# Hash attention and a gated feed-forward block on one core: the first pair of heads is begun in one sweep, and the up products take both halves of the columns under one block of weights

## The chip, the cores and the metric

The kernel runs on one core of one Trainium2 chip. The metric is the device time of one launch in microseconds (us). A core has engines that run their own instruction streams side by side: TensorE (PE in the profile, with the loads of its weights shown apart as PEld), VectorE (DVE), ScalarE (ACT), GpSimd (POOL) and SyncE (SP). Transfers run on 16 DMA engines. SP, ACT and POOL issue them, each into a queue of its own.

## The reference

```python
# attention: batch 4, heads 8, sequence 768, head size 64, 6 hash bits
q_bucket = sum_i ((q @ proj)[..., i] > 0) * 2**i        # k_bucket likewise
scores = where(q_bucket == k_bucket, q @ k.T / 8, -1e9)
attn = exp(scores - max(scores)); attn = attn / (sum(attn) + 1e-9)
x = (attn @ v), heads side by side                      # 3072 x 512
# gated block: d_ff 1536
out = (silu(x @ w_gate) * (x @ w_val)) @ w_out          # 3072 x 512
```

A query attends only to keys that have the same six sign bits.

## The kernel before, in words

**Attention.** Two heads form a pair, and there are 16 pairs, worked one after the other. A pair holds q and k transposed in tiles `qT` and `kT` (128 x 768: two heads of 64 rows each) and their sign bits in `qb` and `kb` (bf16). The 768 queries are two halves of 384 columns, the 768 keys six chunks of 128. A *unit* is one half of the queries against one chunk of keys, for both heads; a pair has 12. `score(u)` takes two PSUM banks, one for each head, and puts two kinds of products in them: `kT` by `qT` (fp32, each product two passes of the array) and on top of these `kb` by `qb` (bf16). The bit product is the mask: the scale is chosen so that only keys with equal bits survive the exponential. Two ACT instructions (L506) then write exp of the unit into `A`. After all 12 units `attend` multiplies `A` with v (L517), and DVE adds the units up for the row sums (L538, L542, L545, called by `add`). `total` sums these over the keys a pair later; the sums go through memory (`few`, `sums`, `r`; SP issues them at L561, L567, L574) and come back as factors.

**Bits.** `hash_blocks` multiplies `hash_w` with `qT` or `kT` (L435) into a bank `hps`, each block of 384 columns in its own 32 rows, and ACT takes the sign (L440). `spread_k` writes the k bits for both heads (L449, two DVE instructions); the q bits are copied to the second head's rows by DVE (L462, first pair) or by a DMA of POOL (L452, later pairs).

**How a pair is prepared.** For the pairs after the first, DVE transposes both operands in 32 x 32 blocks (L473), one pair ahead; for the first, TensorE transposes in 128 x 128 blocks (L422) and ACT copies them out of PSUM (L425). The first pair's preparation is eight steps in a list: transpose k half 0, transpose q half 0, hash k half 0, hash q half 0, and the same for the halves 1. The first four run before any unit. Between the two kinds of products of unit 0 one step runs, between those of unit 1 two more, and after unit 2 the last one. `raw` tiles that q and k are loaded into have one buffer each: the next pair's load waits for this pair's transposes.

**Queues at the start.** SP issues q half 0, k half 1, v, q half 1; ACT issues k half 0; POOL issues `proj`. POOL also clears three bit tiles (L407), and nine idle products (L367) run on TensorE meanwhile. `TURN` (8) is the unit of the first pair after which the second pair's transposes go into DVE's stream and the third pair's loads into SP's.

**PSUM.** Attention has eight banks handed out in turn: a new tile takes the bank of the eighth tile before it and waits for that one's readers.

**Weights.** Between attention's own work the feed-forward weights are split in three parts of few bits each (`begin_pieces`, `advance_pieces`: ACT L135 to L142, DVE L149 to L164). They go to memory and come back in `ring` tiles.

**Gated block.** Three blocks of 1024 tokens, and for each 12 *up* steps and 4 *down* steps. An up step does gate and value: `first` makes 16 products of 128 x 512 into the two banks of `a`, `second` eight into the two banks of `n` (all by `mm`, L669). Each product is a weight load and a matmul. The two banks are the two halves of the tokens (`half`, 512 columns each); ACT or DVE reads both in one instruction of 1024 columns (L708, L714). The order of everything is the order in which the program is written; no planner moves it.

Of the kernel before, what the change touches and what calls it, by code (L numbers as in the profile page):

```python
# [19 lines left out]
def kernel(  # L20
# [20 lines left out]
    nc = tc.nc  # L41
# [256 lines left out]
    def attention(scope):  # L298
# [13 lines left out]
        def fetch(n, name, queue, half=None):  # L312
            b, pr = pairs[n]
            if name == "v":
                t = raws["v", n] = raw.tile([P, 2, NCH, D], FP32, tag="vraw", name="vraw")
                queue.dma_start(
                    t.rearrange("p h c d -> p h (c d)"),
                    v[b, 2 * pr : 2 * pr + 2].rearrange("h (p c) d -> p h (c d)", c=NCH),
                )
                return  # L320
            src = q if name == "q" else k
            if not half:
                raws[name, n] = raw.tile([P, NCH, 2, D], FP32, tag=name + "raw", name=name + "raw",
                                         bufs=1)
            t = raws[name, n]
            if n == 0:
                cs = slice(None) if half is None else slice(half * CH, (half + 1) * CH)
                for h in range(2):
                    queue.dma_start(t[:, cs, h, :],
                                    src[b, 2 * pr + h].rearrange("(p c) d -> p c d", c=NCH)[:, cs, :])  # L330
                return
            blocks = t.rearrange("p c a b -> p (c a b)").rearrange(
                "p (c a d) -> p c a d", a=P // BLOCK, d=BLOCK)
            for h in range(2):
                for x in range(D // BLOCK):
                    at = h * D + x * BLOCK
                    queue.dma_start(
                        blocks[at : at + BLOCK],
                        src[b, 2 * pr + h][:, x * BLOCK : (x + 1) * BLOCK].rearrange(
                            "(a p c) d -> p c a d", c=NCH, p=BLOCK))  # L340
# [6 lines left out]
        two_proj = fixed.tile([P, NBITS], FP32, tag="proj", name="proj")  # L347
        for o in (0, D):
            nc.gpsimd.dma_start(two_proj[o : o + D, :], proj[:, :])
        fetch(0, "q", nc.sync, 0)  # L350
        fetch(0, "k", nc.scalar, 0)
        fetch(0, "k", nc.sync, 1)
        fetch(0, "v", nc.sync)
        fetch(0, "q", nc.sync, 1)

        ident = fixed.tile([P, P], FP32, tag="ident", name="ident")
        make_identity(nc, ident)
# [4 lines left out]
                sides[name, i] = fixed.tile([P, S], BF16, tag=name + f"b{i}", name=name + "b")  # L362
        zeros = sides["k", 1]
        nc.vector.memset(zeros, 0.0)
        for _ in range(9):
            ps = bank("idle")
            nc.tensor.matmul(ps, zeros[:, 0:P], zeros[:, 0:512], start=True, stop=True)  # L367
# [35 lines left out]
            nc.gpsimd.memset(t.rearrange("p u h q -> p (u h) q")[:, :, HQ:AW], 1.0)  # L403
            twos.append(t)
        ring = [t[:, i] for t in twos for i in range(2)]
        for t in (sides["k", 0], sides["q", 0], sides["q", 1]):
            nc.gpsimd.memset(t, 0.0)  # L407

        for name in "kqv":
            fetch(1, name, nc.sync)  # L410
# [3 lines left out]
        bits = {}  # L414

        def front(n):
            def transpose(name, half):
                if (name, n) not in T:
                    T[name, n] = opnd.tile([P, S], FP32, tag=name + "T", name=name + "T")
                ps = bank("tps")  # L420
                for i in range(CH):
                    nc.tensor.transpose(ps[:, i * P : (i + 1) * P],  # L422
                                        raws[name, n][:, half * CH + i, :, :].rearrange("p h d -> p (h d)"),
                                        ident)
                nc.scalar.activation(T[name, n][:, half * HQ : (half + 1) * HQ], ps[:, 0:HQ], AF.Copy,  # L425
                                     scale=2 / OFF if name == "k" else 1.0)

            bits["q", n] = sides["q", n % 2]
            bits["k", n] = sides["k", n % 2]
            low, high = slice(0, BLOCK), slice(D, D + BLOCK)  # L430

            def hash_blocks(todo):
                tile_ = bank("hps")
                for i, (name, half) in enumerate(todo):
                    nc.tensor.matmul(tile_[i * BLOCK : (i + 1) * BLOCK, 0:HQ], hash_w,  # L435
                                     T[name, n][:, half * HQ : (half + 1) * HQ],
                                     start=True, stop=True)

                def sign(i, name, half, to=low, **how):
                    nc.scalar.activation(bits[name, n][to, half * HQ : (half + 1) * HQ],  # L440
                                         tile_[i * BLOCK : (i + 1) * BLOCK, 0:HQ], AF.Sign,
                                         **(how or {"bias": nudge[name]}))

                return [lambda i=i, at=at, **how: sign(i, *at, **how) for i, at in enumerate(todo)]

            def spread_k(times, cols=slice(0, S)):
                b = bits["k", n][:, cols]
                for to, by in ((high, times[1]), (low, times[0])):
                    nc.vector.tensor_scalar(b[to], b[low], scalar1=by, scalar2=None, op0=ALU.mult)  # L449

            def spread_q():
                nc.gpsimd.dma_start(bits["q", n][high], bits["q", n][low])  # L452

            def hash_own(*todo):
                for f in hash_blocks(todo):
                    f()
                for name, half in todo:
                    cols = slice(half * HQ, (half + 1) * HQ)
                    if name == "k":
                        spread_k(mask, cols)  # L460
                    else:
                        nc.vector.tensor_copy(bits["q", n][high, cols], bits["q", n][low, cols])  # L462

            def hash_next(todo):
                q0, q1, *ks = hash_blocks(todo)
                q0()
                q1()
                spread_q()
                return ks + [lambda: spread_k(times_k)]

            def transpose_blocks(name):
                T[name, n] = opnd.tile([P, S], FP32, tag=name + "T", name=name + "T")
                nc.vector.transpose(T[name, n], raws[name, n].rearrange("p c h d -> p (c h d)"))  # L473

            order = [("q", 0), ("q", 1), ("k", 0), ("k", 1)]
            if n:
                return [lambda name=name: transpose_blocks(name) for name in "kq"] + [
                    lambda: hash_next(order)]
            turns = [lambda x=x: transpose(*x) for x in order]
            return [turns[2], turns[0], lambda: hash_own(("k", 0)), lambda: hash_own(("q", 0)),  # L480
                    turns[3], turns[1], lambda: hash_own(("k", 1)), lambda: hash_own(("q", 1))]

        units = [(n, half, c) for n in range(len(pairs)) for half in range(2) for c in range(NCH)]
        acc = {}
# [5 lines left out]
        def weights(u):  # L490
            return ring[u % RING]

        def score(u):
            n, half, c = units[u]
            qs = slice(half * HQ, (half + 1) * HQ)
            ks = slice(c * P, (c + 1) * P)
            sc = [bank("sc")[:, 0:HQ] for _ in range(2)]
            for x, start in ((T, True), (bits, False)):
                if u < 2 and not start:
                    prepare_pair(1 + u)  # L500
                for h in range(2):
                    rows = slice(h * D, (h + 1) * D)
                    nc.tensor.matmul(sc[h], x["k", n][rows, ks], x["q", n][rows, qs],  # L503
                                     start=start, stop=not start)
            for h in range(2):
                nc.scalar.activation(weights(u)[:, h, 0:HQ], sc[h], AF.Exp,  # L506
                                     scale=SCALE * (OFF / 2 if n == 0 else 1.0))

        def attend(u):
            n, half, c = units[u]  # L510
# [75 lines left out]
            if b * S < WB:  # L586
                later.extend(split(x, 0, pr, b * S, min(S, WB - b * S)))

        steps = front(0)
        rest = []  # L590

        def prepare_pair(count):
# [1 line left out]
                if steps:  # L594
                    rest.extend(f for f in steps.pop(0)() or [] if f)

        prepare_pair(4)
        finish(rest)
        last = []
        PACE = [2] * 4 + [1] * 4 + [2, 1] * 4  # L600
        splits = []
        later = []
        TURN = 8
        for n in range(len(pairs)):
            u = 2 * NCH * n
            more = n + 1 < len(pairs)
# [1 line left out]
                steps = front(n + 1)  # L608
                prepare_pair(2)
            for i in range(2 * NCH):  # L610
                score(u + i)
                if u + i == 2:
                    prepare_pair(1)
                    finish(rest)
                    steps = front(n + 1)
                if n == 0 and i == TURN:
                    prepare_pair(2)
                if i % NCH:
# [33 lines left out]
    def gated_block(scope):  # L652
# [18 lines left out]
        def up(F, what):  # L671
# [5 lines left out]
                return w[:, v, j * P : (j + 1) * P]  # L677

            def first():
                for half in range(WB // PIECE):  # L680
                    for j in range(NJ):
                        for v in range(2):
                            mm(a[:, half], block(v, j), r32(xparts[b, j][:, half, v]),
                               j == 0 and v == 0, j == NJ - 1 and v == 1)

            def second():
                for half in range(WB // PIECE):
                    for j in range(NJ):
                        mm(n_[:, half], block(2, j), r32(xparts[b, j][:, half, 2]),
                           j == 0, j == NJ - 1)  # L690

# [213 lines left out]
```

## Time and profile before

| | |
|---|---|
| median of 3 runs | 916.17 us (915.95 to 916.5) |
| profiled execution, its own time | 915.88 us |
| its span, first to last instruction | 914.1 us |
| granted TensorE clock, mean | 0.999 |
| PE busy | 904.9 us (99%) |
| DVE, ACT, POOL busy | 665.5, 455.8, 99.1 us |
| first score product / first product with v / first up product | 7.67 / 22.30 / 319.5 us |

The profile is one execution. Busy shares are of the span. A group's row gives count, busy time, mean duration of one, and idle time of its engine before it. Matmuls overlap in the pipe, so the distance between starts, not the duration, is what one costs. Timelines give start and length in us, and what ended an idle time in brackets.

### The profile page before, as it was taken

How to read it: one execution, taken by the hardware profiler on the slowest of the kernel's cores; microseconds unless marked ns; L12 is line 12 of the kernel's file. 1: busy time of each engine (PE TensorE's matmuls, PEld its weight loads, DVE VectorE, ACT ScalarE, POOL GpSimd, SP SyncE). 2: the span in 40 equal slices, each digit the busy share in tenths (PEclk: the TensorE clock that was granted, in tenths of full speed). 3: DMA queues.
4: the chain of work that ended last, by engine and by line, in shares of the span. 5: the costliest groups of instructions: out<-in, count | busy, mean ns of one | idle time of the engine just before them, and what ended most of it. 6: DMA issues, size and time to landing. Idle time of an engine off the chain costs nothing.

```text
span 914.1 us, 12999 instructions
## 1 busy us (share of the span) xinstructions
PE 904.9 (99%) x4795; PEld 636.9 (70%) x4795; DVE 665.5 (73%) x769; ACT 455.8 (50%) x814; POOL 99.1 (11%) x196
## 2 busy tenths in 40 slices
PE   8999999999999999999999999999999999999997
PEld 3444444444444488888888888888888888888886
DVE  5888999999989768779786856464658754474746
ACT  6889888878888654452414143331313243313230
POOL 2111111011111110000100000101010100001000
PEclk9999999999999999999999999999999999999999
DMA  7677788768886699685756562434434642515232
GB/s 173 138 187 204 190 219 187 181 181 238 233 186 204 204 384 320 221 287 207 291 187 241 199 247 104 175 137 170 140 142 157 236 155 98 191 70 213 98 138 93
DMA packets 145582, 174.28 MB, mean 191 GB/s; under 512 B 106496, under 2 KB 115200, under 8 KB 145520
## 3 DMA queue, kind: packets, MB, share of 16 engines
q0 software_dynamic: 22864, 116.36, 36.1%
q1 hardware_dynamic: 121856, 56.90, 24.2%
q8 instruction: 38, 0.62, 0.3%
q10 hardware_dynamic: 800, 0.20, 0.1%
q14 instruction: 24, 0.20, 0.1%
HBM read 133.17 MB, written 39.42 MB: 189 GB/s over the span
## 4 chain that ended last, share of the span: by engine, by line
PE 96%; DVE 2%; ACT 1%; issue 0%; DVEq 0%; ACTq 0%
PE a L669 29%; PE o L669 19%; PE sc L503 17%; PE n L669 14%; PE av L517 14%; PE hps L435 1%; PE sum L556 1%; ACT A L506 1%; DVE hid L724 0%; DVE hid L722 0%; DVE v L714 0%; DVE v L718 0%; PE idle L367 0%; DVE xparts L292 0%; PE tps L422 0%
## 5 line engine op out<-in xcount | busy, mean ns | idle before, releaser
L669 PE MATMUL a<-xparts,ring 128*128 128x512 f32 x1152 | 273.0, 390 | 0.6 <-ACT row L559 0.6
L669 PEld LDWEIGHTS a<-xparts,ring 128*128 128x128 f32 x1152 | 216.3, 188 | 46.0 <-ACT row L559 1.3
L669 PE MATMUL o<-ring,hid 128*128 128x512 f32 (+1 forms) x870 | 199.0, 389 | 2.3 <-DVE o L795 1.2
L669 PEld LDWEIGHTS o<-ring,hid 128*128 128x128 f32 x870 | 162.5, 188 | 37.1 <-DVE hid L724 2.4
L506 ACT ACTIVATE A<-sc 128x384 f32<-128x384 f32 x384 | 157.0, 492 | 7.6 <-PE sc L503 7.6
L503 PE MATMUL sc<-qT,kT 64*128 64x384 f32 x768 | 156.9, 487 | 0.0
L669 PE MATMUL n<-xparts,ring 128*128 128x512 f32 x576 | 142.3, 390 | 0.0
L517 PE MATMUL av<-A,vraw 128*64 128x386 f32 (+1 forms) x768 | 127.7, 489 | 0.0
L669 PEld LDWEIGHTS n<-xparts,ring 128*128 128x128 f32 x576 | 108.2, 188 | 22.4
L714 DVE TENSOR_TENSOR v<-v,n 128x1024 f32<-128x1024 f32 x36 | 44.0, 1221 | 99.2 <-PE n L669 98.6
L244 POOL DMA_DIRECT2D ring<-ram x108 | 57.0, 529 | 501.1 <-PE n L669 329.1
L517 PEld LDWEIGHTS av<-A,vraw 128*64 128x64 f32 x768 | 53.7, 137 | 73.3 <-issue 61.6
L708 ACT ACTIVATE g<-a 128x1024 f32<-128x1024 f32 x36 | 37.0, 1027 | 132.2 <-PE a L669 127.1
L503 PEld LDWEIGHTS sc<-qT,kT 64*128 64x128 f32 x768 | 67.5, 187 | 48.5 <-issue 47.9
L719 ACT ACTIVATE hid<-v 128x1024 fp32r<-128x1024 f32 x36 | 38.2, 1062 | 115.0 <-DVE v L718 115.0
L716 ACT ACTIVATE g<-g 128x1024 f32<-128x1024 f32 x36 | 38.2, 1062 | 85.2 <-DVE g L714 85.2
L771 DVE TENSOR_TENSOR o<-o 128x512 f32<-128x512 f32 x92 | 63.1, 687 | 20.6 <-ACT o L765 18.2
L714 DVE TENSOR_TENSOR g<-g,n 128x1024 f32<-128x1024 f32 x36 | 43.8, 1216 | 33.2 <-PE n L669 33.2
L503 PE MATMUL sc<-qb,kb 64*128 64x384 bf16 x384 | 63.3, 323 | 0.0
L538 DVE SCALAR_TENSOR_TENSOR both<-A 128x1536 f32<-128x1536 f32 x32 | 55.8, 1744 | 9.2 <-ACT A L506 8.2
L542 DVE TENSOR_TENSOR both<-both,A 128x1536 f32<-128x1536 f32 x32 | 56.3, 1758 | 3.3
L722 DVE SCALAR_TENSOR_TENSOR hid<-hid,v 128x1024 fp32r<-128x1024 f32 x36 | 44.0, 1223 | 19.2 <-ACT hid L719 19.1
(79 smaller groups left out, 702.2 us busy)
## 6 DMA issues: line engine op xcount, KB each, us to landing
ring<-ram POOLq DMA_DIRECT2D x108, 768.0 KB, 4.9
ram<-stage POOLq DMA_DIRECT2D x23, 768.0 KB, 5.6
ram<-stage SPq DMA_DIRECT2D x13, 768.0 KB
qraw<-in_q_dram SPq DMA_DIRECT2D x64, 96.0 KB
vraw<-in_v_dram SPq DMA_DIRECT2D x16, 384.0 KB
kraw<-in_k_dram SPq DMA_DIRECT2D x62, 96.0 KB
out_dram<-o SPq DMA_DIRECT2D x23, 256.0 KB
r<-sums SPq DMA_DIRECT2D x30, 192.0 KB
```

The lines of the kernel that those rows point to most:

```text
L244: nc.gpsimd.dma_start(t.bitcast(FP32), ram[at].bitcast(FP32))
L503: nc.tensor.matmul(sc[h], x["k", n][rows, ks], x["q", n][rows, qs], start=start, stop=not start)
L506: nc.scalar.activation(weights(u)[:, h, 0:HQ], sc[h], AF.Exp, scale=SCALE * (OFF / 2 if n == 0 else 1.0))
L517: nc.tensor.matmul(ps[h * D : (h + 1) * D, 0:width], raws["v", n][:, h, c, :], a[:, h, 0:width], start=c == 0, stop=c == NCH - 1)
L538: nc.vector.scalar_tensor_tensor(out=t, in0=first, scalar=S * EPS / P / 2, in1=now, op0=ALU.add, op1=ALU.add)
L542: nc.vector.tensor_tensor(t, t, now, op=ALU.add)
L669: nc.tensor.matmul(ps, w, x, start=start, stop=stop)
L714: nc.vector.tensor_tensor(two(z), two(z), n_, op=ALU.subtract)
L716: nc.scalar.activation(z, z, AF.Silu)
L719: nc.scalar.activation(h, val, AF.Copy, scale=TOWARD / STEP)
L722: nc.vector.scalar_tensor_tensor(out=l, in0=h.bitcast(FP32), scalar=-STEP, in1=val, op0=ALU.mult, op1=ALU.add)
L771: nc.vector.tensor_tensor(accs[c], accs[c], t[:, 1], op=ALU.subtract)
```

## The change

There are two independent parts.

**The first pair.** q and k halves are all loaded first (q by SP, k by ACT), v after them. The three bit tiles are cleared by DVE right after the first one, not by POOL. A new function `start_first` issues all four transposed halves (k, q, k, q; 12 transposes), k copied out by ACT and q by DVE; then the value products of unit 0; then all four hash products into one bank; signs and spreads of k half 0, q half 0, k half 1; the value products of units 1 and 2; the bit products and exponentials of unit 0; sign and spread of q half 1; bit products and exponentials of units 1 and 2. `score` is divided in `products` and `mark` for this. The loop then scores from unit 3 on. `TURN` becomes 5.

**The up products.** In `first` and `second` the loop over the halves becomes the innermost: each weight block is used for both halves in two products that follow each other.

```diff
-        fetch(0, "q", nc.sync, 0)
-        fetch(0, "k", nc.scalar, 0)
-        fetch(0, "k", nc.sync, 1)
+        for half in range(2):
+            fetch(0, "q", nc.sync, half)
+            fetch(0, "k", nc.scalar, half)
         fetch(0, "v", nc.sync)
-        fetch(0, "q", nc.sync, 1)
...
         nc.vector.memset(zeros, 0.0)
+        for t in (sides["k", 0], sides["q", 0], sides["q", 1]):
+            nc.vector.memset(t, 0.0)
...
-        for t in (sides["k", 0], sides["q", 0], sides["q", 1]):
-            nc.gpsimd.memset(t, 0.0)
...
+            def start_first():
+                for half in range(2):
+                    cols = slice(half * HQ, (half + 1) * HQ)
+                    for name in "kq":
+                        if not half:
+                            T[name, n] = opnd.tile([P, S], FP32, tag=name + "T", name=name + "T")
+                        ps = bank("tps")
+                        for i in range(CH):
+                            nc.tensor.transpose(ps[:, i * P : (i + 1) * P],
+                                                raws[name, n][:, half * CH + i].rearrange("p h d -> p (h d)"),
+                                                ident)
+                        if name == "k":
+                            nc.scalar.activation(T[name, n][:, cols], ps[:, 0:HQ], AF.Copy,
+                                                 scale=2 / OFF)
+                        else:
+                            nc.vector.tensor_copy(T[name, n][:, cols], ps[:, 0:HQ])
+
+                def both_heads(sign, name, half):
+                    cols = slice(half * HQ, (half + 1) * HQ)
+                    sign()
+                    if name == "k":
+                        spread_k(mask, cols)
+                    else:
+                        nc.vector.tensor_copy(bits["q", n][high, cols], bits["q", n][low, cols])
+
+                products(0)
+                todo = [("k", 0), ("q", 0), ("k", 1), ("q", 1)]
+                signs = hash_blocks(todo)
+                for i in range(3):
+                    both_heads(signs[i], *todo[i])
+                products(1)
+                products(2)
+                mark(0)
+                both_heads(signs[3], *todo[3])
+                mark(1)
+                mark(2)
...
-        TURN = 8
+        TURN = 5
...
-                for half in range(WB // PIECE):
-                    for j in range(NJ):
-                        for v in range(2):
+                for j in range(NJ):
+                    for v in range(2):
+                        for half in range(WB // PIECE):
                             mm(a[:, half], block(v, j), r32(xparts[b, j][:, half, v]),
                                j == 0 and v == 0, j == NJ - 1 and v == 1)
...
-                for half in range(WB // PIECE):
-                    for j in range(NJ):
+                for j in range(NJ):
+                    for half in range(WB // PIECE):
                         mm(n_[:, half], block(2, j), r32(xparts[b, j][:, half, 2]),
                            j == 0, j == NJ - 1)
```

More of the change, by code (lines that the diff above doesn't have):

```diff
@@ L326, in fetch @@
             if n == 0:
-                cs = slice(None) if half is None else slice(half * CH, (half + 1) * CH)
+                cs = slice(half * CH, (half + 1) * CH)
                 for h in range(2):
@@ L416, in front @@
         def front(n):
[L417 to L426, printed above, removed]
             bits["q", n] = sides["q", n % 2]
@@ L452, in spread_q @@
                 nc.gpsimd.dma_start(bits["q", n][high], bits["q", n][low])
[L454 to L462, printed above, removed]
             def hash_next(todo):
@@ L478, in front @@
                     lambda: hash_next(order)]
-            turns = [lambda x=x: transpose(*x) for x in order]
-            return [turns[2], turns[0], lambda: hash_own(("k", 0)), lambda: hash_own(("q", 0)),
-                    turns[3], turns[1], lambda: hash_own(("k", 1)), lambda: hash_own(("q", 1))]
+            return start_first()
         units = [(n, half, c) for n in range(len(pairs)) for half in range(2) for c in range(NCH)]
@@ L491, in weights, with product @@
             return ring[u % RING]
-        def score(u):
+        banks_of = {}
+        def product(u, x, start):
             n, half, c = units[u]
@@ L496, in score, with products, mark @@
             ks = slice(c * P, (c + 1) * P)
[L497 to L504, printed above, removed]
-            for h in range(2):
-                nc.scalar.activation(weights(u)[:, h, 0:HQ], sc[h], AF.Exp,
-                                     scale=SCALE * (OFF / 2 if n == 0 else 1.0))
+            for h in range(2):
+                rows = slice(h * D, (h + 1) * D)
+                nc.tensor.matmul(banks_of[u][h], x["k", n][rows, ks], x["q", n][rows, qs],
+                                 start=start, stop=not start)
+        def products(u):
+            banks_of[u] = [bank("sc")[:, 0:HQ] for _ in range(2)]
+            product(u, T, True)
+        def mark(u):
+            product(u, bits, False)
+            for h, sc in enumerate(banks_of.pop(u)):
+                nc.scalar.activation(weights(u)[:, h, 0:HQ], sc, AF.Exp,
+                                     scale=SCALE * (1.0 if units[u][0] else OFF / 2))
+        def score(u):
+            products(u)
+            mark(u)
         def attend(u):
@@ L587, in norm @@
                 later.extend(split(x, 0, pr, b * S, min(S, WB - b * S)))
-        steps = front(0)
         rest = []
@@ L595, in prepare_pair @@
                     rest.extend(f for f in steps.pop(0)() or [] if f)
-        prepare_pair(4)
-        finish(rest)
+        front(0)
+        steps = front(1)
         last = []
@@ L610, in attention @@
             for i in range(2 * NCH):
[L611 to L615, printed above, removed]
+                if u + i > 2:
+                    score(u + i)
                 if n == 0 and i == TURN:
```

## The prediction

> **What bounds the kernel now.** I read the page first, then PE's list of waits, then busy time by stage, then the timelines of the first 22 us, of pairs 5 and 6 and of one up step.
>
> The page, shares and chain:
>
> ```profile
> PE 904.9 (99%) x4795; PEld 636.9 (70%) x4795; DVE 665.5 (73%) x769; ACT 455.8 (50%) x814; POOL 99.1 (11%) x196
> PE 96%; DVE 2%; ACT 1%; issue 0%; DVEq 0%; ACTq 0%
> PE a L669 29%; PE o L669 19%; PE sc L503 17%; PE n L669 14%; PE av L517 14%; PE hps L435 1%; PE sum L556 1%; ACT A L506 1%; DVE hid L724 0%; DVE hid L722 0%; DVE v L714 0%; DVE v L718 0%; PE idle L367 0%; DVE xparts L292 0%; PE tps L422 0%
> ```
>
> TensorE is the bound. 4795 matmuls have 4795 loads. The stages, in columns of busy us (instructions) for PE, PEld, DVE, ACT, POOL, then clock, DMA share and GB/s:
>
> ```profile
> 4.80:22.30 17.50, 15.87 (x101) 7.28 (x101) 9.92 (x14) 13.61 (x32) 1.12 (x2) 1.00 0.74 186
> 22.30:30.20 7.90, 7.90 (x52) 3.35 (x48) 7.34 (x11) 5.16 (x10) 1.30 (x2) 1.00 0.67 112
> 100.00:120.00 20.00, 20.00 (x144) 9.57 (x142) 19.16 (x24) 17.35 (x40) 2.38 (x4) 1.00 0.77 175
> ```
>
> From 22.3 on PE never stops; only the first pair has holes. Whatever brings the first product with v (22.30) forward moves everything behind it, as far as DVE (19.16 of 20 us there) and the DMAs keep up. The first pair:
>
> ```profile
> 6.26 0.14 PEld L435 LDWEIGHTS hps<-kT,hash 128*32 128x32 f32 x2 [0.79 <-ACT kT L425]
> 6.29 0.81 PE L435 MATMUL hps<-kT,hash 128*32 128x384 f32 x2 [0.58 <-ACT qT L425]
> 6.94 0.81 PE L435 MATMUL hps<-qT,hash 128*32 128x384 f32 x2
> 9.00 0.34 PE L503 MATMUL sc<-qb,kb 64*128 64x384 bf16 x2
> 21.51 0.52 PE L435 MATMUL hps<-qT,hash 128*32 128x384 f32 x2 [0.98 <-ACT A L506]
> 22.30 0.54 PE L517 MATMUL av<-A,vraw 128*64 128x386 f32 x2
> ```
>
> One hash block alone costs 0.64 us of PE (6.29 to 6.94), four in one bank together go through in 0.78 (21.51 to 22.30). The 0.98 ahead of 21.51 is put down to ACT; what ends then is DVE's transpose of q for pair 1 (20.43 + 0.93).
>
> Two later places where PE is nearly late, pair 6 and pair 5:
>
> ```profile
> 125.85 0.85 DVE L449 TENSOR_SCALAR kb<-kb,columns 32x768 bf16<-32x768 bf16 x2
> 127.10 0.33 PE L503 MATMUL sc<-qb,kb 64*128 64x384 bf16 x2
> ...
> 106.38 0.85 DVE L449 TENSOR_SCALAR kb<-kb,columns 32x768 bf16<-32x768 bf16 x2
> 107.87 0.33 PE L503 MATMUL sc<-qb,kb 64*128 64x384 bf16 x2
> ...
> 86.97 0.23 DVE L565 RECIPROCAL few<-few 128x12 f32<-128x12 f32 x1 [1.38 <-DMA few<-row]
> ```
>
> The k bits are ready 0.40 and 0.64 us before PE takes them, and from 86.97, where DVE had waited for a DMA, to 126.7 DVE has no idle time. And one up step:
>
> ```profile
> 603.16 3.79 PE L669 MATMUL a<-xparts,ring 128*128 128x512 f32 x16
> 606.79 1.98 PE L669 MATMUL n<-xparts,ring 128*128 128x512 f32 x8
> 608.60 7.64 PE L669 MATMUL o<-ring,hid 128*128 128x512 f32 x33
> L367 PEld LDWEIGHTS <-kb x9: 98/151/151, 1.3 to 4.2; 128*128 128x128 bf16 x9
> ```
>
> 3.63 us for 16 and 1.81 for 8: 226.7 ns each, whether the bank changes or not. The last line is nine products in a row by one and the same block of zeros: nine loads.
>
> [...] the two copies of 64 x 6 at 5.09 took 1.06 us while POOL cleared bit tiles[...].
>
> **The change part by part.** Times of before, unless "new".
>
> *Up products.* 1728 matmuls and 1728 loads before, the same after, if loads aren't dropped. ACT and DVE read both halves at once, so what they wait for still ends last at the same place; the operands of j = 3 are wanted later than before (product 13, not 7). Spacing across a bank change equals the spacing inside a bank. Cost 0. Bounds, unseen: 1 ns a matmul either way is 1.7 us.
>
> *Loads and clearing.* ACT issues two more DMAs (0.5 each), so its table load ends near 4.2 instead of 3.1; ACT is first needed at 5.42, which hides it (0 even if 1 us more). Three memsets on DVE of 0.38 like the one at 0.89: DVE idles until 3.66 and hides them. [...] the hash weights, in use at 6.26 before, are wanted at 7.46 new. v lands later than before, but isn't wanted before 19. k half 0 and q half 0 keep their place: transposes start at 4.87. k and q halves 1: before, k half 1 was used as soon as 8.52 and shows no landing; from the spacing of the issues (0.5 us, second in each queue) and the sharing I estimate 5.7 to 6.1 and take 6.0.
>
> *The walk, new.* PE: six transposes 4.87 to 5.55 (0.36 for three), k half 1 at 6.13, q half 1 at 6.49, free at 6.82. ACT copies k (0.49) by 5.91 and 7.2. DVE copies q: no such row; 512 columns from PSUM take 0.68 (o, L767), so 384 about 0.55. [...] I take 0.55: ready at 6.3 and 7.54. Value products of unit 0 (0.645: two passes of 0.32 with the heads side by side; with 0.16 for the bits this makes the steady 0.807 a unit that 9.73 us for 12 show at 30.2): 6.82 to 7.46. Four hash blocks side by side from 7.46, the last held by q to 7.66: its second pass begins 7.98, PE is free at 8.30. Value products of units 1 and 2 end at 9.59. Signs (0.58 each) start 0.59 after the last pass: 8.57, 9.15, 9.73. That takes it that a sign waits for all four blocks; by its own it would be 0.23 earlier. DVE spreads k (0.69) by 9.86, copies q (0.25) by 10.11; bits of units 0 to 2 run 10.25 to 10.73 on PE (before: 9.00). Exponentials: unit 0 at 10.61 (0.36 after its bits), then one each 0.37; the sign of q half 1 lies between (0.57), units 1 to 3 are at 11.93 to 14.27.
> PE from here waits for banks: unit 3 wants the bank of unit 0's first head (11.2), unit 4 that of the hash (12.0), unit 5 those of unit 1 (12.9), 6 and 7 follow at 13.66 and 14.47. From unit 7 on PE runs its own 0.807 a unit: end 18.50.
> Pair 1's hash needs DVE: L538 of unit 3 from 14.3 (before 15.0), 1.86; then, as TURN is 5, the two transposes, done 18.0; raw q of pair 1, loaded 2.4 us earlier than before (SP from 6.7, not 9.1), is there by 15. So hash at 18.50, v products at 18.50 + 0.78 = 19.28: **3.0 us earlier**. With the kinder ends (landing 5.7, own sign) 3.55; with landing 6.5, 2.6.
>
> Where it comes from: hash blocks 4 x 0.64 - 0.84 = 1.7; q copies off ACT and the interleaved waits (PE idles about 1.6 in 4.8:22.3) the rest.
>
> *Does it last?* The next waits are DVE's and SP's. DVE is unbroken from 14.3 to the transposes of pair 2, which end 0.7 earlier than before (32.3 to 31.6); it waited there for ACT until 34.70, now 31.7, so DVE joins in with the 3.0. SP loads pair 3 from the transposes on, 0.7 earlier; behind these loads stands the row sum `few` (issued 41.55; SP was free at 40.73): new 40.05, and with 2.0 to 2.4 us from issue to use (63.62 to 66.06, 84.92 to 86.97) it is there at about 42.3, against 44.98 - 3.0 for DVE's reciprocal. So DVE comes out 2.6 to 2.7 earlier, and keeps that through transposes, loads, `few` and the unbroken stretch to 126.7. At pair 6 PE needs its k bits: 2.6 plus 0.25 of the 0.40 (0.15 is the least from DVE's end to PE, 21.37 to 21.51) is **2.85**. After that no margin is under 1 us.
>
> 915.88 - 2.85 = 913.0 for the profiled execution; this is 0.29 under the median of runs, so 913.3.
>
> **Rivals.**
> 1. *The DMA loop doesn't come along.* Transfers of pairs 3 to 6 collide otherwise than before (DMA 95% busy in 48 to 65), `few` lands only 0.7 to 1.8 earlier. Gain 0.95 to 2.0: 914.2 to 915.2. For: the spacing of the pairs' transposes, 21 to 22.6 us in pairs 3 to 5 against PE's 19.23. Against: DVE's idle 2.4 us at 32.3 and SP's 0.8 at 40.7.
> 2. *Weight loads are dropped* for the second of two equal blocks[...]. Against: nine loads at L367.
> 3. *Slower: two open banks by turns cost the array.* Every up matmul pays x ns; 1.65 ns cancels the gain, 2.7 ns makes it slower by 0.2%; 5 ns gives 921.9. For: the trace has no run of alternating banks. Against: 226.7 at each bank change that it has.
> 4. *All of the first pair's gain stays*: `few` early enough and the kinder ends, 3.3 to 3.8: 912.4 to 912.9.
>
> **How the numbers follow.** The forecast (912.9 to 914.2) has 0.58, rival 1 0.18, rival 2 0.04, rival 3 0.09, rival 4 0.11. Three runs spread 0.06%; about 0.2% (1.83 us, under 914.34) tells from no change. Faster: 0.58 + 0.04 + 0.11 and a fifth of rival 1, 0.77; same 0.14; slower 0.09. The range from 912.2 (rival 4 less the runs' spread) to rival 1's 915.2 leaves out rivals 2 and 3.
>
> **What would show it.** First v product near 19.3; four hash blocks within 0.9 us; first exponential near 10.6, later than before's 9.49; up matmuls still 226.7 with 4795 loads; the k bits of pair 6 with no more than 0.2 to spare, or a PE wait there. Wrong if the halves 1 land after 6.5, if PE waits before 40 us for a transpose or bank, or if 16 products of `a` don't take 3.63.

## The result and the profile after

The changed kernel takes 914.2 us, the median of 13 runs (913.98 to 915.82); the kernel before, run beside it, takes 916.18 us (915.95 to 916.65). The medians differ by 1.98 us, 0.22%, which is 0.9 us less than the 2.85 us forecast. The ratio taken over all runs is 0.9981, with a 95% interval from 0.9973 to 0.999: a gain of 0.19%, just at the bound of 0.2% that the prediction drew. Three more sets of runs below, in which at most a part without effect was undone, give 0.9978 to 0.9979.

The profiled execution took 914.08 us, with a span of 912.0 us. From the page, the busy shares and the chain of work that ended last, by engine:

```profile
PE 904.2 (99%) x4795; PEld 638.8 (70%) x4795; DVE 667.2 (73%) x774; ACT 453.8 (50%) x812; POOL 97.0 (11%) x193
PE 97%; DVE 2%; DMA 0%; ACTq 0%; ACT 0%; issue 0%; DVEq 0%
```

TensorE is still the bound, and there are still 4795 loads for 4795 matmuls. The stages by windows of the changed kernel (busy us and instructions of PE, PEld, DVE, ACT, POOL, then clock, DMA share, GB/s; the clock column shows 1.00 also for the time before the clock was first granted, which the trace's clock records put at 6.04 us):

```profile
4.80:20.14 15.34, 15.04 (x102) 9.55 (x101) 8.30 (x14) 11.70 (x29) 0.00 (x0) 1.00 0.83 203
20.14:28.05 7.91, 7.91 (x52) 3.35 (x48) 7.38 (x10) 5.79 (x13) 0.52 (x1) 1.00 0.82 129
98.00:118.00 20.00, 20.00 (x144) 9.52 (x142) 19.16 (x24) 17.13 (x40) 2.52 (x5) 1.00 0.73 184
```

The first stage is 15.34 us where it was 17.50, with one PE instruction more in it; the products with v take the same 7.9 us, and in mid-attention PE is as full as before. The first pair in the timeline (start, length, engine, line, what; in brackets the idle time before it and what ended it). Lines from several engines are put together in order:

```profile
5.13 0.85 PE L461 MATMUL tps<-ident,kraw 128*128 128x128 f32 x3
...
6.70 0.52 PE L461 MATMUL tps<-ident,kraw 128*128 128x128 f32 x3 [0.30 <-DMA kraw<-in_k_dram]
7.06 0.49 PE L461 MATMUL tps<-ident,qraw 128*128 128x128 f32 x3
7.48 0.92 PE L514 MATMUL sc<-qT,kT 64*128 64x384 f32 x4
7.58 0.56 DVE L468 COPY qT<-tps 128x384 f32<-128x384 f32 x1 [0.59 <-PE tps L461]
8.32 0.51 PE L423 MATMUL hps<-kT,hash 128*32 128x384 f32 x1
...
8.34 0.51 PE L423 MATMUL hps<-qT,hash 128*32 128x384 f32 x1
...
9.11 0.59 PE L514 MATMUL sc<-qT,kT 64*128 64x384 f32 x2
...
11.09 0.87 ACT L524 ACTIVATE A<-sc 128x384 f32<-128x384 f32 x2
...
19.36 0.52 PE L423 MATMUL hps<-qT,hash 128*32 128x384 f32 x2
...
20.14 0.54 PE L539 MATMUL av<-A,vraw 128*64 128x386 f32 x2
```

The first product with v is at 20.14 us, 2.16 us earlier than before (22.30). The transposes of k half 1 start at 6.70, at the end of a wait for its DMA. The four hash blocks start together at 8.32 to 8.34 (the first and the last are shown), 0.84 us after the value products of unit 0; DVE's copy of q half 1 is ready at 7.58 + 0.56 = 8.14, 0.18 before.

All of the 2.16 us last to the end in this profile: the first up product comes at 317.34 us (before 319.49), and the span is 2.1 us shorter. At pair 6 the k bits still come in time. From the timeline of the changed kernel there, and of one up step:

```profile
123.81 0.85 DVE L437 TENSOR_SCALAR kb<-kb,columns 32x768 bf16<-32x768 bf16 x2
...
124.95 0.33 PE L514 MATMUL sc<-qb,kb 64*128 64x384 bf16 x2
...
601.08 3.79 PE L687 MATMUL a<-xparts,ring 128*128 128x512 f32 x16
604.71 1.98 PE L687 MATMUL n<-xparts,ring 128*128 128x512 f32 x8
```

The bits are ready at 123.81 + 0.85 = 124.66, 0.29 us before PE takes them (0.40 before). Sixteen products of `a` take 604.71 - 601.08 = 3.63 us, as before, 227 ns each.

### The profile page after: what moved, and what is told of

Read it like the earlier page. It is cut to its first block, busy times and chain, and to the rows that moved or that the text cites. A ratio compares the mean times of both kernels' runs of the same rounds, so it can differ in the third digit from the quotient of the medians.

```text
span 912.0 us, 12995 instructions
## 1 busy us (share of the span) xinstructions
PE 904.2 (99%) x4795; PEld 638.8 (70%) x4795; DVE 667.2 (73%) x774; ACT 453.8 (50%) x812; POOL 97.0 (11%) x193
## 4 chain that ended last, share of the span: by engine, by line
PE 97%; DVE 2%; DMA 0%; ACTq 0%; ACT 0%; issue 0%; DVEq 0%
PE a L687 29%; PE o L687 20%; PE sc L514 17%; PE n L687 14%; PE av L539 14%; PE sum L578 1%; PE hps L423 1%; DMA kraw<-in_k_dram 0%; DVE hid L742 0%; DVE hid L740 0%; DVE v L732 0%; DVE v L736 0%; DVE xparts L292 0%; ACTq L329 0%; ACT hid L737 0%
## 5 line engine op out<-in xcount | busy, mean ns | idle before, releaser
L514 PEld LDWEIGHTS sc<-qT,kT 64*128 64x128 f32 x768 | 70.3, 187 | 47.8 <-issue 41.9
L514 PE MATMUL sc<-qb,kb 64*128 64x384 bf16 x384 | 66.0, 323 | 0.0
```

The costliest lines, as they stand in the source:

```text
L514: nc.tensor.matmul(banks_of[u][h], x["k", n][rows, ks], x["q", n][rows, qs], start=start, stop=not start)
```

## The experiments

Each kernel was run beside the kernel before, whose median was 916.21 to 916.24 us throughout. Edits are to the changed kernel unless it says otherwise.

### The two parts apart

The kernel before, with the loops of the up products alone turned round:

```diff
 def first():
-    for half in range(WB // PIECE):
-        for j in range(NJ):
-            for v in range(2):
+    for j in range(NJ):
+        for v in range(2):
+            for half in range(WB // PIECE):
```

> The kernel before with the up products' new loop order alone. If the order costs nothing (the theory): 916.2 us, within 0.1% of before, 16 products of a in 3.63 us, 4795 loads. If alternating banks or repeated weights matter (rivals 2 and 3 of the prediction): 907 or less, or 918 or more.

The changed kernel with the old order of the up products (the same lines turned back):

> The changed kernel with the up products' old loop order: the first pair's part alone. Theory: the same as the changed kernel, 914.0 to 914.3 us, first product with v near 20.1. If the loop order carried part of the gain: 915 or more.

The up order alone takes 916.38 us, ratio 1.0002 (0.9994 to 1.001). The pair alone takes 914.09 us, 0.9979 (0.9972 to 0.9987), with its first product with v at 20.03. The timeline of the first kernel, one up step:

```profile
601.96 1.98 PE L669 MATMUL n<-xparts,ring 128*128 128x512 f32 x8
603.77 3.56 PE L669 MATMUL a<-xparts,ring 128*128 128x512 f32 x15
```

Eight products of `n` take 603.77 - 601.96 = 1.81 us with the bank changing at every product, as without. The whole gain is the first pair's.

### Why the first pair gave less than forecast

The first v product is 0.86 us later than forecast (20.14, not 19.28). Two readings were left by the profile. In (a) the halves 1 land late. In (b) the clock counts: by the clock records of the traces it was granted at 6.04 us in this profile and at 4.06 in that of before, so the idle products and the first transposes ran slower (three transposes have 0.85 us at 5.13, and 0.52 at 6.70). The changed kernel was run again unchanged, for another profile:

> The changed kernel once more, for a second profile. Two readings of why 914.2 and not 913.3: (a) k half 1 lands at 6.5 us in every run, then the first product with v comes at 20.0 to 20.2 again, whenever the clock is granted; (b) the late grant of the clock (6.0 us in the profile after, 4.1 before) did it: then a run with an early grant has it at 19.4 to 19.6 and is 0.6 us shorter.

It takes 914.07 us, 0.9978 (0.9969 to 0.9986). Here the clock was granted 0.53 us earlier, at 5.51, and the list of PE's waits shows the time given back to the same DMA, 0.2 us more of it than in the first profile:

```profile
PE tps L461 <- DMA kraw<-in_k_dram: 0.5, 1, 0.5
```

The first v product is at 20.10. The clearest case is in a profile of the kernel with `TURN` 8 and another `PACE` (below), where the clock was granted early again, at 4.37. From its timeline:

```profile
4.82 0.52 PE L461 MATMUL tps<-ident,kraw 128*128 128x128 f32 x3
...
6.57 0.52 PE L461 MATMUL tps<-ident,kraw 128*128 128x128 f32 x3 [0.90 <-DMA kraw<-in_k_dram]
...
8.19 0.51 PE L423 MATMUL hps<-kT,hash 128*32 128x384 f32 x1
```

The transposes start at 4.82, as forecast, and PE then waits 0.90 us for k half 1. So (a) holds and (b) falls: an earlier start of the first transposes only makes a longer wait for the landing. A late clock does count once the landing is past. In the profile of the first kernel with another `PACE` (below) it was granted only at 7.30, no wait for the DMA is left, and the first v product is at 20.44. In the changed kernel the two limits lie close together: PE, slower until 6.04, was through with q half 0 at 5.78 + 0.62 = 6.40, so an earlier landing alone would have won only the 0.30 us of the wait.

The loads alone put back in their old order (k half 1 behind q half 0 on SP, then v, then q half 1):

```diff
-for half in range(2):
-    fetch(0, "q", nc.sync, half)
-    fetch(0, "k", nc.scalar, half)
+fetch(0, "q", nc.sync, 0)
+fetch(0, "k", nc.scalar, 0)
+fetch(0, "k", nc.sync, 1)
 fetch(0, "v", nc.sync)
+fetch(0, "q", nc.sync, 1)
```

> The changed kernel with the old order of the first loads (k half 1 on SP behind q half 0, then v, then q half 1). Theory: the landing of the later of the halves 1 sets the first pair. q half 1 lands near 7.4 to 7.6 instead of 6.4, all four hash blocks wait for it, the first product with v comes at 20.7 to 21.0 (20.1) and the time is 914.7 to 915.0. If the half 1 is hidden behind other work: 914.1.

It takes 915.38 us, 0.9993 (0.9985 to 1.0002). The profiled execution, at 914.77, is within the forecast; the median is 0.4 us above it, and what lengthens the slower executions was not traced. The timeline (lines are one further down here):

```profile
7.78 0.52 PE L462 MATMUL tps<-ident,qraw 128*128 128x128 f32 x3 [0.52 <-DMA qraw<-in_q_dram]
...
9.08 0.51 PE L424 MATMUL hps<-kT,hash 128*32 128x384 f32 x1
```

q half 1 now lands behind v. Its transposes start at 7.78 where the changed kernel's start at 7.06, 0.72 later; the hash blocks move back by 0.76, and the first v product by 0.76 to 20.90. The walk follows the start of the last transposes nearly one to one.

The four hash blocks each in a bank of its own, one after another, instead of side by side in one bank:

```diff
-signs = hash_blocks(todo)
+signs = [hash_blocks([x])[0] for x in todo]
```

> The changed kernel with the four hash products in a bank each, all in the same 32 columns of the array. Theory: they run one after the other, 4 x 0.64 us instead of 0.78 together; the first product with v comes 1.4 to 1.8 us later, near 21.7, and the time is 915.5 to 915.9. If the four in one bank save nothing because TensorE waits for ACT's signs there: 914.1 to 914.5.

It takes 915.53 us, 0.9993 (0.9984 to 1.0001). The timeline:

```profile
7.98 0.83 PE L423 MATMUL hps<-kT,hash 128*32 128x384 f32 x2
8.65 0.81 PE L423 MATMUL hps<-qT,hash 128*32 128x384 f32 x2
9.30 0.81 PE L423 MATMUL hps<-kT,hash 128*32 128x384 f32 x2
9.94 0.81 PE L423 MATMUL hps<-qT,hash 128*32 128x384 f32 x2
10.68 0.59 PE L514 MATMUL sc<-qT,kT 64*128 64x384 f32 x2
```

From the first block to the product after them is 2.70 us, against 9.11 - 8.32 = 0.79 in the changed kernel: side by side is worth 1.9 us of PE. Of this, 1.1 us reaches the first v product (21.24), since exponentials and banks set part of the walk, and it would be more at equal landing (k half 1 was there earlier, at 6.23, in this profile). The first block starts 7.98 - 7.14 = 0.84 us after the value products here too, though alone it needs nothing of q half 1; these 0.84 are taken up below.

The clearing of the three bit tiles given back to POOL:

```diff
-for t in (sides["k", 0], sides["q", 0], sides["q", 1]):
-    nc.vector.memset(t, 0.0)
 ...
+for t in (sides["k", 0], sides["q", 0], sides["q", 1]):
+    nc.gpsimd.memset(t, 0.0)
```

> The changed kernel with the three bit tiles cleared by POOL where they were before. The prediction put this edit at nothing: POOL's clearing holds up DVE's copies of the hash weights by 0.9 us at most, to 6.2 to 6.5, and the hash starts at 8.2 to 8.3: 914.0 to 914.3. If it delays the first transposes or the copy of q out of PSUM: 914.5 or more.

914.21 us, 0.9979 (0.997 to 0.9989), first v product 20.14, no change. The timeline has the copies of the hash weights longer, and hidden all the same:

```profile
4.93 1.26 DVE L393 COPY hash<-proj 64x6 f32<-64x6 f32 x2 [0.48 <-DMA proj<-in_proj_dram]
```

In the changed kernel these two copies take 0.16 and 0.17 us; in the one before they take 1.06 together (5.09 to 6.15), while POOL clears bit tiles (3.85 to 5.92). So they are longer in both of these profiles, where POOL clears; what held them up was not shown. With the clears on DVE (0.89 to 2.49), POOL issues `proj` at 1.26 as before. The hash products, which need these copies, start only at 8.26 us.

### Whether the gain can be kept, and what `TURN` does

```diff
-TURN = 5
+TURN = 8
```

> The changed kernel with TURN at 8 again. Theory: DVE has the transposes of pair 1 ready only after the adds of units 5 and, with them, near 21.2 us; the hash of pair 1 waits for it, the first product with v comes at 22.0 to 22.2 and the gain is nearly all gone: 915.9 to 916.2 us. If the transposes' place doesn't matter: 914.2.

It takes 917.65 us, 1.0012 (1.0005 to 1.0019), slower than before. The timeline shows the expected wait:

```profile
21.60 0.52 PE L423 MATMUL hps<-qT,hash 128*32 128x384 f32 x2 [2.11 <-DVE qT L451]
```

PE stands 2.11 us for DVE's transpose of pair 1, and the first v product is back at 22.38. That is the whole gain: six of the 18 runs are at 916.1 to 916.5 us, near the kernel before. The profiled one is at 916.83, and eleven are at 917.5 to 918.8, 1.4 us and more above the quickest. The first thought was that these lose 1.4 us in waits at pairs 5 and 6, where the margins are thin: this kernel's profile has such a wait, of 0.3 us at pair 6. `PACE` says how many pieces of weight splitting each pair takes on; with less splitting in the early pairs DVE has room there. Two kernels tried that, without and with `TURN` 8:

```diff
-PACE = [2] * 4 + [1] * 4 + [2, 1] * 4
+PACE = [2] * 3 + [1] * 7 + [2] * 5 + [1]
```

> The changed kernel, with the same 24 weight pieces handed out otherwise: 2 for each of pairs 0 to 2, 1 for pairs 3 to 9, 2 for 10 to 14, 1 for 15 (before: 2 for 0 to 3, 1 for 4 to 7, then 2 and 1 by turns). Theory: the runs of the changed kernel over 914.4 us are waits for the k bits of pairs 5 and 6, where DVE has 0.3 to 0.5 us to spare; with some 3 us less DVE work ahead of them the margins go over 2 us, the quickest runs stay at 913.9 and the slow ones go: median 913.9 to 914.0, highest under 914.4. If the slow runs come from the start (the clock's grant, landings): the spread stays, up to 915 and more.

> TURN at 8 and the pieces handed out as in the run before with that. TURN at 8 alone took 917.65, though its first product with v came at 22.38, as late as the kernel before's, which takes 916.2. Theory: the other 1.4 us are waits at pairs 5 and 6; they go with the lighter pairs: 916.1 to 916.2. If they lie elsewhere: 917 and more.

They take 931.02 us (1.0163, 1.0149 to 1.0176) and 934.35 us (1.0194, 1.018 to 1.0208). The margins at pairs 5 and 6 rose to 1.7 and 2.6 us in the first of them and to 2.8 and 3.7 in the second, and no wait is left in pairs 1 to 11; but the pieces moved to pairs 12 to 15 stop ACT. From the list of PE's waits in the first of them (us in total, times, longest):

```profile
PE sc L514 <- ACT xT L549: 9.0, 4, 3.2
```

and from ACT's:

```profile
ACT stage L135 <- DMA ram<-stage: 12.9, 2, 7.2
```

ACT stands at L135 for a staging tile that is still on its way to memory, behind it stand its exponentials and copies, and PE waits 9.0 us for these. In two stretches behind these waits, of 3.41 and 6.83 us, the clock is at 0.50, which by half of these costs another 5.1 us of PE at most, an estimate. Some 14 of the 16.4 us between the two profiled executions (930.46 and 914.08) are named so; the rest was not traced. The second kernel shows something else besides, in the windows around its 2.1 us wait:

```profile
18.00:21.40 3.40, 1.30 (x11) 0.61 (x7) 3.37 (x5) 2.99 (x8) 0.00 (x0) 1.00 0.83 271
21.45:24.80 3.35, 3.35 (x14) 0.91 (x16) 3.21 (x3) 1.78 (x4) 0.39 (x1) 0.50 0.49 77
25.00:28.00 3.00, 3.00 (x22) 1.25 (x18) 2.88 (x5) 3.00 (x5) 0.00 (x0) 1.00 0.94 149
```

After the wait the granted clock is half for 3.41 us, and the stretch of 3.35 us has 14 PE instructions. The kernel with `TURN` 8 and the smaller move below has 24 in the same stretch, at full clock:

```profile
21.45:24.80 3.35, 3.17 (x24) 1.31 (x26) 3.25 (x3) 2.20 (x4) 0.52 (x1) 1.00 0.41 65
```

By half of these 3.41 us, I estimate that the half clock costs 1.7 us of PE. A smaller move of the pieces, one less in pair 3, took the waits at pairs 5 and 6 away without that damage, for the changed kernel, for it with `TURN` 8, and for the kernel before:

```diff
-PACE = [2] * 4 + [1] * 4 + [2, 1] * 4
+PACE = [2] * 3 + [1] * 5 + [2, 1] * 4
```

> The changed kernel with one weight piece fewer at pair 3 (1, not 2): 23 pieces in attention, the rest is left to the gated block, which has room on DVE and ACT. It keeps the run of two-piece pairs short, unlike the earlier run on this, where two pieces a pair at a stretch made ACT wait for a stage tile. Theory (thin margins at pairs 5 and 6): k bits there 2 us or more ahead, no PE wait there, quickest runs 913.9, median 913.9 to 914.1 and no run over 914.5. If the spread comes from the start: runs up to 915 or more remain.

> TURN at 8 and one piece fewer at pair 3. TURN at 8 alone took 917.65, with the first product with v at 22.38. Theory: the 1.4 us over the kernel before are waits at pairs 5 and 6 and go: 916.1 to 916.3. If they lie elsewhere: 917 and more.

> The kernel before with one piece fewer at pair 3. Theory: its quickest runs (915.9) hardly move, since TensorE then waits nowhere in pairs 1 to 15; its median (916.2) comes down by at most 0.3, to 915.9 to 916.0, with fewer runs over 916.4. If the piece itself costs time in attention: 915.5 or less; if it costs in the gated block: over 916.3.

| kernel | median, range (us) | ratio (95%) | margin at pairs 5, 6 |
|---|---|---|---|
| changed, this `PACE` | 914.54 (914.43 to 915.05) | 0.998 (0.9972 to 0.9989) | 2.1, 3.0 |
| the same, `TURN` 8 | 916.93 (916.7 to 918.41) | 1.0011 (1.0003 to 1.0019) | 3.5, 4.4 |
| before, this `PACE` | 916.95 (916.68 to 917.31) | 1.0007 (0.9999 to 1.0015) | 2.8, 3.7 |

Three things follow. First, with `TURN` 8 the runs still fall in two groups, eight at 916.7 to 916.95 and five at 918.23 to 918.41, though the margins are far from used up. So the thought that the 1.4 us are waits at pairs 5 and 6 falls. The clock that is recorded for every run tells the groups apart: its mean is 0.997 or 0.998 in all sixteen longer executions of the two kernels with `TURN` 8 (917.5 and up), and 0.999 or 1.0 in fourteen of the other fifteen (one has 0.998). Half a clock for 3.41 us out of some 916 lowers the mean by 0.0019 and costs 1.7 us, so it has both sizes. That it stands behind the 2.1 us wait is seen in the one profile only.

What may set the struck executions apart can be read from the clock records. In these traces the stretch between two changes of the clock is a whole multiple of 3.413 us: 904.53 us in the changed kernel is 265 of them and 907.95 in the one before 266, 40.96 between the two half stretches of the first kernel with another `PACE` is 12, 17.07 from the grant to the half clock in the second is 5, and a half stretch is 1 or 2. So the changes seen here lie on a grid of that step. The first grants, at 4.06 us before, 6.04 in the changed kernel and 7.30 in the first kernel with another `PACE`, show that the grid lies differently in each execution. Where the 2.1 us wait fell into a single step (18.02 to 21.44 in the profile above), PE was busy for 1.3 us of it and half clock followed. Where a step boundary divided it (19.73 to 23.14 in the profile of `TURN` 8 alone), the emptier step still had 1.5 us and full clock followed. If the grid lies evenly and either figure is the limit, I estimate from these figures that 38 to 50% of executions are struck; sixteen of 31 were. That there is such a limit was not shown.

Second, the spread narrows: ten of eleven runs of the changed kernel with this `PACE` lie within 0.4 us, where six of the thirteen without this edit stand 0.6 to 1.8 us above the quickest. That speaks for these runs losing their excess to waits at pairs 5 and 6; their recorded clock is no lower than that of the quick ones. Waits there were seen in the profiles of three variants: the serial hash (0.4 and 0.6 us, both at pair 5), the up order alone and `TURN` 8 (0.3 us at pair 6 each). But no run of the changed kernel itself with such a wait was profiled, so this cause is not shown.

Third, the quickest runs are 0.5 us slower than the changed kernel's. With fewer pieces split in attention, one piece more is left to the gated block, and there a new wait stands in PE's list, of this `PACE` in the changed kernel:

```profile
PE o L687 <- DVE o L789: 0.4, 1, 0.4
```

In the kernel before, too, the quickest runs lose by this edit (916.68, not 915.88). So none of these beats the changed kernel.

## Why the prediction was right or wrong

**Right: the up products cost and give nothing.** They take 227 ns each with 4795 loads after, and 1.0002 alone. Rival 2 (loads dropped) and rival 3 (alternating banks cost) are excluded. **Right: clearing at no cost**, and the copy of q on DVE: estimated 0.55, measured 0.56. **Right: the four hash blocks side by side**: 0.84 us estimated from their start to PE's freedom, 0.79 measured; signs 0.6 us after the last pass, as taken. The kinder end, in which a sign waits only for its own block, can't be told from the other here: the four blocks ran together, with their last passes through between 9.16 and 9.18, and the first sign starts at 9.29. **Right: `TURN` 5 is needed**: without it PE waits 2.11 us, the whole gain. **Right for the gain that there was: DVE's and SP's loop comes along.** Pair 6 lets the 2.16 us pass, with 0.29 left. But DVE came 2.0 us earlier, not 2.6 to 2.7, and it waited for `few`:

```profile
84.97 0.23 DVE L587 RECIPROCAL few<-few 128x12 f32<-128x12 f32 x1 [1.30 <-DMA few<-row]
```

Before, this was at 86.97. Had PE been 2.85 us earlier and DVE no earlier than here, pair 6 would have held PE at 124.66 + 0.15 = 124.81 (0.15 us from DVE's end to PE, as the prediction takes it) and the gain at 127.10 - 124.81 = 2.29, an estimate from this profile. Whether DVE would then have come earlier stays open: in the profile of the pair alone it is at 83.83. Rival 1 named the measured time, 914.2, but not for its reason: in the profile nothing is lost between 20 us and the end. Rival 4, that all of the first pair's gain stays, had the mechanism, on a larger gain than there was. "From 22.3 on PE never stops" leaves out PE's waits at the gated block (1.2, 1.1 and 0.6 us in its list of waits), which are the same after.

**Wrong in size: "k half 0 and q half 0 keep their place ... k and q halves 1 ... I estimate 5.7 to 6.1 and take 6.0."** This is the term that failed, and most of what is missing. k half 1 is there at 6.56, and its transposes start at 6.70 where 6.13 was forecast: 0.57 us. The prediction named a landing past 6.5 as what would make it wrong, and that happened. The estimate came from the spacing of the issues and a guess at the sharing. The eight loads of q and k, 0.79 million bytes together, are issued between 0.74 and 2.9 us, and v's 0.39 million at 3.72. From 1.80 to 6.56 us the windows have the DMA engines full at 235 GB/s, which is 1.12 million bytes: when k half 1 was in, at least 0.33 million of v had moved as well. So v shared the engines with it; how early it would land without v was not run. In the six profiles with these loads in which PE waits for k half 1, it landed between 6.2 and 6.6. The term also hid a second one: the forecast start of 4.87 is the one before, with its early clock. With the clock at 6.04 some 0.27 of the 0.57 would have stayed (6.40, not 6.13) however early k half 1 had landed.

**Wrong in part: "Value products of unit 0 (0.645 ...): 6.82 to 7.46 ... the last held by q to 7.66".** 0.645 us is their cost in a row of units. Between operations on all 128 rows they cost more here, and the trace of before had the row. From its timeline, with the start of the next operation under each:

```profile
7.67 0.92 PE L503 MATMUL sc<-qT,kT 64*128 64x384 f32 x4
8.52 0.55 PE L422 MATMUL tps<-ident,kraw 128*128 128x128 f32 x3
...
13.90 0.81 PE L503 MATMUL sc<-qT,kT 64*128 64x384 f32 x4
14.55 0.33 PE L503 MATMUL sc<-qb,kb 64*128 64x384 bf16 x2
```

0.85 us from start to start in the first, 0.65 in the second. With one such neighbour it was 0.75 (from 30.21 to 30.96, behind products with v). After the change it is 0.84, with the hash blocks side by side or one after another, and the weight load of the first hash block starts with it at 8.32, not ahead. The step before also grows: from q's transposes to the value products it is 7.48 - 7.06 = 0.42, where three transposes followed by others take 0.36. What TensorE does between such neighbours was not shown; both of these steps around unit 0 together took some 0.3 us more (0.06 and 0.20) than in a row of their own kind. The hold for q is then no term of its own: the copy is ready 0.18 us before the blocks start, and 0.85 was there before the change without such a copy.

The chain in numbers, forecast to measured, from the start of k half 1's transposes: late by 0.57; the six transposes to the value products 0.69 to 0.78, 0.09 more; these to the hash 0.64 to 0.84, 0.20 more; the hash to PE free 0.84 to 0.79, 0.05 less. Together 0.81: PE is free at 9.11, not 8.30. The 0.81 does not simply run on. The first exponential is only 0.48 late (11.09, not 10.61), as the bits had come closer behind the signs; but the exponentials of unit 0 and the sign behind them took longer than forecast, those of unit 1 are 0.66 late (12.59, not 11.93), and the hash of pair 1 and the first v product 0.86. The bound "with landing 6.5, 2.6" was too kind by 0.4: by its own sum it is 3.02 - 0.50 = 2.5, and the steps around unit 0 are another 0.24 (0.09 + 0.20 - 0.05).

**Not reached: "At pair 6 ... 2.85".** The limit that was to trim 3.0 to 2.85 did not bind in the profile, as the first pair brought less. Its tightness is real (0.29 us left), and is likely, though not shown, what makes some runs slower.

**In sum**: 2.85 forecast, less 0.86 of the walk, plus 0.15 that was not trimmed, is 2.14; the profile shows 2.16 at the first v product and 2.1 in the span, and 915.88 - 914.08 = 1.8 between the two profiled executions' own times. The medians give 1.98. The measured 914.2 is the very end of the band 912.9 to 914.2 that the forecast was given: the mechanism was right, and the first pair's gain was put too high.

## What to carry to other kernels

When a preparation is put in one sweep, the last operand to land can set its pace (here transposes that start 0.72 us later moved the first v product by 0.76), so price the landing by the whole line of transfers that shares the DMA engines, at its late end (here k half 1 at 6.56 us, with at least 0.33 million bytes of v moved by then); do the walk again from there, not with a discount. Hash products that use 32 columns of TensorE are worth putting side by side (0.79 us for four, 2.70 one after another), and look up in the trace what products on half the rows cost beside products on all of them: here 0.1 us more for each such neighbour than in a steady row (0.65, 0.75 and 0.85 us with none, one and two). A gain won at the start reaches the end only when the next engine's preparations are drawn forward with it: here by `TURN` 5, worth the whole gain. And a wait can cost more than its length: here 2.1 us, with an estimated 1.7 us of half clock behind it in one of three profiles.

## What the runs showed of the hardware

A TensorE wait of 2.1 us was followed by 3.41 us at half the granted clock in one of the three profiles that have it, that of `TURN` 8 with the larger move of the pieces; in the other two, `TURN` 8 alone and with the smaller move, the clock behind the wait is 1.00. How the wait lay in the grid of 3.413 us tells that profile and `TURN` 8 alone apart. Where PE was busy for 1.31 us of a step (18.02 to 21.44 there) or 1.26 (242.82 to 246.23 with the larger move alone), half clock followed; where it was busy for 1.54 (19.73 to 23.14 with `TURN` 8 alone), full clock. At the end of the kernel before and of the changed one, steps with 1.01 and 0.98 us (from 908.59 and 907.16) were followed by half clock, and earlier ones with 2.77 (from 318.08 and 316.65) by full. One half stretch lasted two steps, 6.83 us, with PE busy for 6.12 of the 6.70 us from 290.70 to 297.40.

The same fp32 products (two for each head in the trace, where the bf16 ones have one) cost 0.65 us in a row of units and 0.85 when operations on all 128 rows stand on both sides (both in the trace of before). This was there to be read before the change, and not looked for.
